# Retention and a low-rank mixer on one core: seven products for batch 1's second layer, fifteen sections instead of sixteen, another order in the front

## The chip, the cores and the metric

The kernel runs on one core of one Trainium2 chip. The metric is the device time of one execution, in microseconds. Before the change it is 306.77 us, the median of 3 runs (305.24 to 308.22). The names of the engines in the profile: PE is TensorE, PEld its weight load, DVE is VectorE, ACT is ScalarE, POOL is GpSimd, SP is SyncE, which here only starts DMAs.

## The reference

Eight batches, eight heads, 576 positions, head dimension 64, all float32. First a retention layer (attention without softmax, with a decay for each head), then a mixer over the sequence and a two-layer network over the channels:

```python
scores = scale * np.matmul(q, k.transpose(0, 1, 3, 2))
Dmat = np.where(rel >= 0, gamma[:, None, None] ** rel[None, :, :], 0.0)
x = np.matmul(scores * Dmat[None], v)            # then heads side by side: (8, 576, 512)
...
h = x.transpose(0, 2, 1) @ U @ V                 # rank 32, over the sequence
u = x + h.transpose(0, 2, 1)
out = u + np.maximum(u @ w_ch1, 0.0) @ w_ch2     # 512 -> 2048 -> 512
```

## The kernel before

**Chunks.** Two batches have 1152 rows, nine chunks of 128; the fifth chunk of such a pair (number J = 4) holds the last 64 rows of the even batch and the first 64 of the odd one. `order` numbers all 36 chunks of the four pairs, 0 to 35. The program calls a batch `b`, its pair `pr` and its place in the pair `par`.

**Retention.** The decay is folded into q and v by two scales, so a chunk needs its own masked scores and a running state. Chunks 0 to 8 (batches 0 and 1) are made by hand in `front`, in "units" of 256 rows with on-chip transposes: `cast_u` and `scale_u` bring q, k and v to bf16, `T_pe` transposes on TensorE, `T_cp` copies the result out of PSUM, `SC_u` makes scores, `mask_u` masks them, `RV_u` and `QS_u` make the output, `XS_u` scales it into the tile x. Chunks 9 to 35 go through a pipeline: `load` (SyncE queue, into the pool `stage` of 15 buffers; a chunk takes three), `prep` (cast of k, scale of q and v, and a transposing DMA on SyncE's queue), and then a **section**. `section(new, last)` makes the scores and the state increments of the chunks of group `new` and the outputs of the group before (`last`): four lists of 64x64 matmuls, lines 319, 336, 405 and 416. After it come `mask` (line 355: three operations on VectorE for a group of two chunks, four for one) and `cast_states` (line 384).

**Mixer.** `mixer_items` makes U and V products (`MA`, `MH`) and adds them to x as u; `MT` transposes u.

**Network.** Y1 (line 559) multiplies u by w1 in blocks of 128 columns with four matmuls of up to 512 columns each, and ScalarE takes the ReLU. Y2 (line 765) makes a chunk of 128 rows by 16 matmuls of 128x512, VectorE adds u (line 771) and GpSimd's queue stores it. Where `parted` is true (today pairs 1 to 3), four chunks are taken together and split in halves in every direction, and Y2's eight half-size products become seven (Strassen's scheme, in Winograd's form): `product` in `y2_items` (line 810), 16 matmuls of 128x256 for each. They need eight sums S of parts of y1 (`s_sum`, line 739) in every batch and eight sums T of parts of w2 (`t_sums`, line 599) once, all on VectorE, and corrections afterwards: `after` copies a bank on ScalarE (line 828), adds on VectorE (847, 854) and adds u on GpSimd (line 832). Banks A, B and C live in the three-buffer pool `ps_big`, which Y1, sections and the mixer use too. An odd batch keeps its chunk J as a whole chunk.

**Order.** Nothing is scheduled by a planner: the program runs under `manual_schedule`, each engine takes its instructions in the order in which the program issues them. `front` is written out. From then on a batch's main work is a list of items with costs (Y1 and Y2 items, in TensorE columns), and `merge` (line 16) issues steps between them: `plan[b]` gives a letter and a share of the batch's cost for each step. S is a section, M its mask, C its cast of states, L the loads of a chunk's k and q, K of its v, P (and Q, O) its preparation with k cast on GpSimd (VectorE, ScalarE), W and V a swap of v, G a mixer item, A an S sum, T a T sum, R and X sums for the last batch, F a pair of rows of w2 (`gated_w2`, which waits for a block of y1). Batch 1's list begins with what `front` leaves of Y1 (ten blocks) and then holds Y2 of batch 0 and of batch 1:

```python
main = y1_left + y2_items(0, 0) + y2_items(0, 1)
```

`groups` (line 1483) says how many chunks each section takes: (1, 2, 2, 1, 2, 1) and then twice (2, 2, 1, 2, 2), sixteen groups for 27 chunks.

Of the kernel before, what the change touches and what calls it, by code (L numbers as in the profile page):

```python
# [30 lines left out]
def kernel(  # L31
# [17 lines left out]
    P = 128  # L49
# [667 lines left out]

    P_ORDER = ((0, 0), (1, 0), (0, 1), (1, 1), (2, 0), (2, 1), (3, 0), (3, 1))
# [23 lines left out]
    def y2_items(pr, par):  # L742
# [47 lines left out]
        def product(n, e):  # L790
# [10 lines left out]
                4: ("A", False, y[:, hi, c + 2 * P:c + 4 * P],  # L801
# [15 lines left out]
        def after(n):  # L817
# [7 lines left out]
            copied = {1: ("A", lo[:, :, L]), 6: ("A", lo[:, :, H_]), 5: ("C", hi[:, :, H_])}  # L825
            if n in copied:
                bank, to = copied[n]
                nc.scalar.activation(out=to, in_=st[bank], func=AF.Copy)  # L828
# [24 lines left out]
            if n == 4:  # L853
                nc.vector.tensor_tensor(
                    out=hi[:, :, L], in0=st["A"], in1=u_hi[:, :, L], op=ALU.add)
            if last_b and n == 4:
                store(hi, L, nc.sync)
            elif not last_b and n in (3, 4):
                store(lo if n == 3 else hi, slice(0, dm), nc.gpsimd)

        parted = pr > 0
# [7 lines left out]
        if parted:  # L869
            for n in (1, 2, 6, 5, 7, 3, 4):  # L870
# [356 lines left out]
    def front():  # L1227
# [77 lines left out]
        cast_J(HI, POOL, (1,))  # L1305
        cast_J(HI, POOL, (0,))
        load_w1(2)
# [75 lines left out]
        T_cp(2, 1, DVE)  # L1383
        T_pe(2, 0)
        T_cp(2, 0, DVE)
        ys[7]()
# [7 lines left out]
        ys[9]()  # L1394
        cast_u(3, 1, 0, POOL)
        cast_u(3, 1, 1, POOL)
        load_w1(3)
        cast_u(3, 0, 0, POOL)
        cast_u(3, 0, 1, POOL)
        load(*order[NI], (1, 0, 2), gate=True)  # L1400
        load(*order[NI + 1], (1, 0, 2))
        scale_u(3, 0, POOL)
        scale_u(3, 1, POOL)
        T_pe(3, 1)
        T_cp(3, 1, DVE)
        ys[10]()
# [11 lines left out]
        load(*order[NI + 2], (1, 0, 2))  # L1418
        load_w2(0)
        load_w2(2)  # L1420
        load_w2(4)
# [7 lines left out]
        warm(3, ps_big, "big")  # L1429
        MA1(steps=(0, 3))  # L1430
# [7 lines left out]
        XS_u(3, 1, 2)  # L1438
        to_xT(1, (0, 1), (5, 6))
        ys[14]()  # L1440
        to_xT(1, (0, 1), (7,))
        MA1(steps=(3, J))
# [9 lines left out]
        prep(NI)  # L1452
# [24 lines left out]
    with tc.manual_schedule():  # L1477
# [5 lines left out]
        for size in (1, 2, 2, 1, 2, 1) + 2 * (2, 2, 1, 2, 2):  # L1483
# [120 lines left out]
```

## Time and profile before

| | |
|---|---|
| median of 3 runs | 306.77 us (305.24 to 308.22) |
| profiled execution | 306.29 us |
| its span, first to last instruction | 304.5 us |
| granted TensorE clock | 1.000 |
| DMA, mean over the span | 175 GB/s, 53.35 MB |
| queue of SyncE, share of 16 engines' time | 62.5% |
| queue of GpSimd, the same | 16.0% |
| chain that ended last | PE 88%, DMA 7%, SyncE's queue 3% |
| batch 2's first Y1 matmul starts | 105.57 us |

A row of a group reads: line, engine, operation, tiles (out<-in), shape, how many | busy time, mean ns of one | idle time of the engine just before them, and who ended it. A row of the timeline reads: start, duration of the run of equal instructions, engine, line, operation, tiles, shape, count, and in brackets the wait before it. The chain's rows are start, duration, what, count. Matmuls are pipelined, so a mean duration of one is longer than the spacing of two; the spacing is read from runs of equal matmuls.

### The profile page before, as it was taken

The numbers are of one execution on the slowest core, as the hardware profiler recorded it, in microseconds if no ns is written. First come the engines' busy times: TensorE is split into PE (matmuls) and PEld (weight loads), VectorE is DVE, ScalarE is ACT, GpSimd is POOL, SyncE is SP. The second block draws the span as 40 slices with busy tenths as digits, with TensorE's granted clock in tenths as the row PEclk, the third lists the DMA queues.
The fourth block names the chain that finished last, engine by engine and source line by source line (L and its number), as shares of the span: only waits on it lengthen the run. The fifth ranks groups of instructions, "written<-read, shape, count | busy, mean of one in ns | idle before, by whom it ended". The sixth has DMA issues, their size and how long they took to land.

```text
span 304.5 us, 9953 instructions
## 1 busy us (share of the span) xinstructions
PE 296.6 (97%) x4268; PEld 197.9 (65%) x4276; DVE 209.0 (69%) x373; ACT 156.4 (51%) x321; POOL 139.4 (46%) x173
## 2 busy tenths in 40 slices
PE   8799999999999999999999999999999999999996
PEld 3565564554554444887768845887758745887885
DVE  7863764633678986889269487787589528867763
ACT  3647456662424286447872376367842375226510
POOL 6672864463264475437620486259342400550130
PEclk9999999999999999999999999999999999999999
DMA  6999899999999999899978699959774033030013
GB/s 198 284 189 260 238 203 219 202 232 195 269 211 255 247 243 215 151 177 301 220 157 166 147 230 205 196 136 297 139 167 111 5 140 86 2 125 15 1 54 121
DMA packets 150268, 53.35 MB, mean 175 GB/s; under 512 B 128880, under 2 KB 148208, under 8 KB 150224
## 3 DMA queue, kind: packets, MB, share of 16 engines
q1 hardware_dynamic: 143616, 40.40, 62.5%
q0 software_dynamic: 6608, 12.32, 16.0%
q8 instruction: 33, 0.54, 0.7%
q14 instruction: 11, 0.09, 0.1%
HBM read 36.85 MB, written 9.44 MB: 152 GB/s over the span
## 4 chain that ended last, share of the span: by engine, by line
PE 88%; DMA 7%; SPq 3%; issue 1%; POOL 0%; DVE 0%; POOLq 0%
PE ps_y L559 34%; PE ps_A L810 14%; PE ps_y L765 12%; PE ps_C L810 7%; PE ps_B L810 3%; DMA stage_t<-in_q_dram 3%; PE ps_yA L680 3%; SPq L1220 2%; DMA stage_t<-in_v_dram 2%; DMA stage_t<-in_k_dram 2%; PE po L405 2%; PE psc L319 1%; PE po L416 1%; PE ph L497 1%; PE ps_y L780 1%; PE ps_yC L680 1%
## 5 line engine op out<-in xcount | busy, mean ns | idle before, releaser
L559 PE MATMUL ps_y<-uT,w 128*128 128x512 bf16 (+3 forms) x632 | 111.6, 331 | 0.0
L565 ACT ACTIVATE y<-ps_y 128x512 bf16<-128x512 f32 (+3 forms) x158 | 75.6, 500 | 40.3 <-PE ps_y L559 39.8
L559 PEld LDWEIGHTS <-w 128*128 128x128 bf16 x632 | 57.4, 98 | 42.6 <-issue 0.5
L832 POOL TENSOR_TENSOR o_lo<-o_lo,u 128x512 f32<-128x512 f32 x12 | 17.4, 1452 | 61.8 <-DVE o_lo L847 41.5
L810 PEld LDWEIGHTS <-S 128*128 128x128 bf16 x384 | 37.0, 98 | 4.7
L765 PE MATMUL ps_y<-w_sb,y 128*128 128x512 bf16 x168 | 38.4, 379 | 0.8 <-issue 0.6
L265 POOL TENSOR_TENSOR qk<-stage_t,qscale 128x512 bf16<-128x512 f32 x27 | 28.7, 1064 | 20.0 <-DMA stage_t<-in_q_dram 17.7
L275 POOL TENSOR_TENSOR vt<-stage_t,vscale 128x512 bf16<-128x512 f32 x27 | 29.7, 1098 | 15.6 <-DMA stage_t<-in_v_dram 14.5
L739 DVE TENSOR_TENSOR S<-y 128x1024 bf16<-128x1024 bf16 x24 | 20.6, 864 | 18.3 <-ACT y L565 18.3
L355 DVE TENSOR_TENSOR ret<-psc,triX 64x512 bf16<-64x512 f32 (+2 forms) x53 | 31.0, 585 | 1.0
L810 PEld LDWEIGHTS <-y 128*128 128x128 bf16 x288 | 27.8, 98 | 4.1
L765 PEld LDWEIGHTS <-y 128*128 128x128 bf16 x176 | 16.5, 98 | 19.2
L503 DVE TENSOR_TENSOR u<-ph,xt 128x512 bf16<-128x512 f32 (+4 forms) x33 | 22.4, 733 | 5.5 <-PE ph L497 5.2
L425 ACT ACTIVATE xt<-po 128x512 bf16<-128x512 f32 x27 | 14.9, 595 | 20.1 <-PE po L416 19.7
L377 DVE TENSOR_TENSOR s_f<-inc,s_f 128x256 f32<-128x256 f32 x38 | 16.1, 424 | 10.7 <-PE inc L336 9.0
L810 PE MATMUL ps_A<-T,S 128*128 128x256 bf16 x192 | 23.3, 273 | 0.0
L828 ACT ACTIVATE o_lo<-ps_A 128x512 f32<-128x512 f32 x12 | 7.2, 597 | 28.2 <-PE ps_A L810 23.6
L384 ACT ACTIVATE s_sb<-s_f 128x1024 bf16<-128x1024 f32 (+1 forms) x16 | 14.7, 921 | 8.9 <-DVE s_f L377 8.1
L1017 POOL CAST qk<-stage_t 128x512 bf16<-128x512 f32 (+1 forms) x21 | 13.4, 639 | 12.5 <-DMA stage_t<-in_k_dram 12.5
L1017 DVE COPY vs<-vt 64x256 bf16<-64x256 bf16 x32 | 15.5, 486 | 0.5
L832 POOL TENSOR_TENSOR o_hi<-o_hi,u 128x512 f32<-128x512 f32 x6 | 7.1, 1176 | 14.8 <-DVE o_hi L847 14.2
L905 POOL CAST qk<-stage_t 128x512 bf16<-128x512 f32 x16 | 9.7, 617 | 8.7 <-DMA stage_t<-in_k_dram 5.9
(173 smaller groups left out, 430.3 us busy)
## 6 DMA issues: line engine op xcount, KB each, us to landing
stage_t<-in_q_dram SPq DMA_DIRECT2D x32, 256.0 KB
stage_t<-in_k_dram SPq DMA_DIRECT2D x30, 256.0 KB
stage_t<-in_v_dram SPq DMA_DIRECT2D x30, 256.0 KB
out_dram<-o_lo POOLq DMA_DIRECT2D x5, 512.0 KB, 4.5
out_dram<-o_hi POOLq DMA_DIRECT2D x5, 512.0 KB, 5.5
w<-in_moe_w_ch_dram POOLq DMA_DIRECT2D x4, 512.0 KB, 7.6
w_sb<-in_moe_w_ch_dram POOLq DMA_DIRECT2D x8, 256.0 KB, 6.0
out_dram<-o POOLq DMA_DIRECT2D x8, 256.0 KB, 3.7
```

The lines of the kernel that those rows point to most:

```text
L265: nc.gpsimd.tensor_tensor(out=t[:, 0, :].rearrange("p (h d) -> p h d", d=D), in0=c["f", 0], in1=qscale[:, i, :, None].to_broadcast([P, H, ...
L275: (eng or nc.gpsimd).tensor_tensor(out=c["v"][rows], in0=c["f", 2][rows], in1=vscale[rows, i, :, None].to_broadcast([n, H, D]), op=ALU.mult,)
L355: nc.vector.tensor_tensor(out=ret[to, n, 0:m], in0=psc[rows, bank, 0:m * D].rearrange("p (b i) -> p b i", i=D), in1=tri_m[rows], op=ALU.mult,)
L377: nc.vector.tensor_tensor(out=s_f[:, s, :], in0=src, in1=s_f[:, st["f_end"], :], op=ALU.add)
L503: nc.vector.tensor_tensor(out=st["u", par][:, i0 - base:i0 - base + n, w].rearrange("p s (c d) -> p c s d", c=len(ccs)), in0=t[:, :, 0:n, ...
L559: nc.tensor.matmul(ps[:, 0:n, :], w1_t[f * P // W1B][:, cc, f * P % W1B:f * P % W1B + P], st["uT", par][:, c0:c0 + n, cc, :], start=(cc == ...
L565: nc.scalar.activation(out=st["y1", par][:, f, c0 * P:(c0 + n) * P], in_=ps[:, 0:n, :].rearrange("p s t -> p (s t)"), func=AF.Relu)
L739: nc.vector.tensor_tensor(out=t[:, k, js], in0=in0, in1=in1, op=op)
L765: nc.tensor.matmul(ps, st["y1", par][:, f, c * P:(c + 1) * P], w2_sb[:, f, :], start=(f == 0), stop=(f == NF - 1),)
L810: nc.tensor.matmul(st[bank][:, e, :], a[:, j, e * P:(e + 1) * P], w(j), start=(first and e == 0 and j == 0), stop=True, skip_group_check=True,
L832: nc.gpsimd.tensor_tensor(out=o[:, :, w], in0=o[:, :, w], in1=u[:, :, w], op=ALU.add)
L1017: eng.tensor_copy(out=out, in_=in_)
```

## The change

1. **Sections.** The group sizes become (1, 2, 2, 1), six times 2, and (2, 2, 1, 2, 2): fifteen groups. Chunks 17 and 18, which were in two groups, form one.
2. **Batch 1's Y2 in seven products.** `parted` becomes true for `par == 1` of pair 0. There the order of products is 1, 2, 4, 6, 5, 7, 3 instead of 1, 2, 6, 5, 7, 3, 4 (`early4`): product 4 goes to a bank D of its own, which ScalarE copies out, and is added after product 7. Batch 1 gets eight S sums (A steps, order `P1_ORDER`); the T sums start at the head of its plan and end before product 7, in another order.
3. **Front.** One load of w1 (`load_w1(2)`) is issued one cast earlier on GpSimd, `load_w1(3)` two casts earlier; `ys[7]` and `ys[10]`, blocks of four Y1 matmuls of batch 0, go ahead of transposes; unit 3's scales go ahead of the gated loads of chunk 9; `warm(3)` becomes `warm(2)`; the mixer's first three steps move behind unit 3's outputs; chunk 9's `prep` comes earlier, and the loads of w2 rows 2 to 5 and of chunk 11 come behind it.
4. **Steps at other places.** The plans of batches 1 to 7 are new.

```diff
+    P1_ORDER = ((0, 0), (1, 0), (0, 1), (1, 1), (2, 0), (2, 1), (3, 0), (3, 1))
...
-                4: ("A", False, y[:, hi, c + 2 * P:c + 4 * P],
+                4: ("D" if early4 else "A", early4, y[:, hi, c + 2 * P:c + 4 * P],
...
+            if early4:
+                copied[4] = ("D", hi[:, :, L])
...
-            if n == 4:
+            if early4 and n == 7:
+                nc.vector.tensor_tensor(
+                    out=hi[:, :, L], in0=st["A"], in1=hi[:, :, L], op=ALU.add)
+                add_u(hi, L, u_hi)
+            elif not early4 and n == 4:
...
-            elif not last_b and n in (3, 4):
+            elif not last_b and n in (3, 7 if early4 else 4):
...
-        parted = pr > 0
+        parted = pr > 0 or par == 1
+        early4 = pr == 0
...
-            for n in (1, 2, 6, 5, 7, 3, 4):
+            for n in (1, 2, 4, 6, 5, 7, 3) if early4 else (1, 2, 6, 5, 7, 3, 4):
...
+        load_w1(2)
         cast_J(HI, POOL, (0,))
-        load_w1(2)
...
+        ys[7]()
         T_pe(2, 0)
         T_cp(2, 0, DVE)
-        ys[7]()
         ys[8]()
...
+        load_w1(3)
         cast_u(3, 1, 0, POOL)
         cast_u(3, 1, 1, POOL)
-        load_w1(3)
         cast_u(3, 0, 0, POOL)
         cast_u(3, 0, 1, POOL)
+        scale_u(3, 0, POOL)
+        scale_u(3, 1, POOL)
         load(*order[NI], (1, 0, 2), gate=True)
         load(*order[NI + 1], (1, 0, 2))
-        scale_u(3, 0, POOL)
-        scale_u(3, 1, POOL)
+        ys[10]()
         T_pe(3, 1)
         T_cp(3, 1, DVE)
-        ys[10]()
...
-        load(*order[NI + 2], (1, 0, 2))
         load_w2(0)
-        load_w2(2)
-        load_w2(4)
...
-        warm(3, ps_big, "big")
-        MA1(steps=(0, 3))
+        warm(2, ps_big, "big")
         RV_u(3, 0)
...
         XS_u(3, 1, 2)
+        prep(NI)
+        load_w2(2)
+        load_w2(4)
+        load(*order[NI + 2], (1, 0, 2))
...
-        MA1(steps=(3, J))
+        MA1(steps=(0, J))
...
-        prep(NI)
         load_w2(6)
...
-        for size in (1, 2, 2, 1, 2, 1) + 2 * (2, 2, 1, 2, 2):
+        for size in (1, 2, 2, 1) + 6 * (2,) + (2, 2, 1, 2, 2):
...
-        t_order = [(k, half) for k in range(4) for half in range(2)]
+        t_order = [(k, half) for k in (0, 1, 3, 2) for half in range(2)]
...
-            sums = list(P_ORDER if b == B - 1 else S_ORDER) if pr else []
+            sums = list(P_ORDER if b == B - 1 else P1_ORDER if b == 1 else S_ORDER)
```

The plan of batch 1, where most of it happens, before and after:

```diff
-            1: ("F.039 Q.0726 S.118 L.1736 K.1753 W.1802 F.1823 W.1901 C.2583 P.2585 "
-                "Q.3063 L.3157 L.3468 M.3469 K.3698 V.4225 S.4276 K.434 O.4367 M.4856 "
-                "K.5071 P.5251 C.537 S.5581 M.5838 L.6099 W.6207 C.6783 T.6854 L.7 T.7065 "
-                "S.71 K.7122 P.7196 G.7368 M.745 T.7709 G.79 K.8049 T.8077 V.8107 T.8113 "
-                "T.8127 G.82 L.8681 C.886 S.8982 C.9003 M.9187 P.9275 T.9908 T.9999 L.9999"),
+            1: ("T.0 P.0589 F.0605 W.0983 S.0993 C.1498 T.1532 W.1651 L.1861 K.2046 F.235 "
+                "T.2987 Q.3063 L.3175 P.3195 K.32 K.3453 M.3662 T.3778 V.405 L.4124 T.4155 "
+                "S.4253 C.4565 L.4586 O.478 K.4803 M.4813 V.5075 T.5174 P.532 S.5364 L.5583 "
+                "M.5702 A.624 T.6291 K.6343 A.663 A.6639 C.6784 A.682 S.6961 M.7072 P.7167 "
+                "G.7711 K.7756 G.8009 C.8265 K.8283 A.8351 L.8393 A.8421 A.846 A.8584 "
+                "T.8796 S.8854 G.8872 L.8906 Q.9066 Q.9163 C.9228 V.9554"),
```

In batch 2's plan the first section stands at S.1186 (before: S.2131) and takes chunks 17 and 18.

39 rows, old and new, of the table plan are left out of this document.

## The prediction

> **What bounds the kernel now.** I read the page first, then who made TensorE wait, then the chain that ended last, and only then the other engines' rows at the places that the change touches.
>
> ```profile
> span 304.5 us, 9953 instructions
> ## 1 busy us (share of the span) xinstructions
> PE 296.6 (97%) x4268; PEld 197.9 (65%) x4276; DVE 209.0 (69%) x373; ACT 156.4 (51%) x321; POOL 139.4 (46%) x173
> ```
>
> ```profile
> PE pw L216 <- POOL ident masks.py:199: 1.4, 1, 1.4
> PE pst L920 <- POOL qk L905: 1.1, 3, 0.5
> PE ps_y L765 <- issue: 0.6, 4, 0.2
> ```
>
> The first fence says that TensorE is hardly ever free. The second is the list of its waits, longest first: one wait for the identity at the start, waits for casts in the front, and four gaps of about 0.16 us ahead of Y2's matmuls, which no other engine causes. So outside the front the order of TensorE's own instructions sets the end, and an edit is worth what it takes from, or adds to, that queue. What other engines do counts only once it is late.
>
> The chain (start, length, what, how many instructions) shows the two rates that matter, and what a section and the mixer's steps take:
>
> ```profile
> 33.10 1.73 PE ps_y L559 x8
> ...
> 90.57 0.30 PE po L405 x20
> 91.66 1.67 PE ps_y L765 x7
> 93.34 0.39 PE pa L461 x20
> 93.73 1.83 PE ps_y L765 x8
> 95.56 0.34 PE ph L497 x16
> ...
> 123.92 1.75 PE ps_B L810 x16
> ```
>
> Eight products of 128x512 take 1.73 us, 0.216 each (Y2's whole chunks have the same shape; some of their records are missing, so I take the rate from this row). Sixteen of 128x256 take 1.75 us, 0.109 each. A section with one new chunk lasts from 90.57 to 91.66, 1.1 us; the mixer's first product takes 0.39, its second 0.34.
>
> **Part 1: batch 1's Y2.** Today five chunks of 16 matmuls of 128x512. After: one such chunk, then seven products of 16 matmuls of 128x256. Removed: 64 x 0.216 = 13.8 us. Added: 112 x 0.109 = 12.2 us. TensorE saves 1.6 us. The four gaps before L765 stand after a section or a mixer step that interrupts a whole chunk; two of the four (the one ahead of 91.66, and the one behind the mixer's second product) lie in the part that becomes products, and L810's rows show no such gap, so I take off 2 x 0.16 = 0.3 more. Bounds: 1.6 to 2.0.
>
> The Trainium skill, TensorE: Matmul & The Clock Gate, section "Back-to-back issue gap", gives for a stream of weight loads and matmuls a sustained 131 ns at 512 columns and 81 ns at 128; worked out by it (an estimate, with some 98 ns at 256 between the two), 64 x 0.131 = 8.4 us would go and 112 x 0.098 = 11.0 us would come, and the change would cost 2.6 us. The rows above contradict it at both widths, and agree with the formula that the same section gives for a single gap; the rows decide.
>
> **What the seven products ask of VectorE.** They need eight sums S (line 739) in batch 1, and the eight sums T (line 599), which today end at 110 us, done before product 7.
>
> ```profile
> L739 DVE TENSOR_TENSOR S<-y 128x1024 bf16<-128x1024 bf16 x24 | 20.6, 864 | 18.3 <-ACT y L565 18.3
> ...
> L739 DVE TENSOR_TENSOR S<-y,S 128x1024 bf16<-128x1024 bf16 x12 | 8.0, 681 | 0.1
> ```
>
> ```profile
> 85.00:106.00 21.00, 20.63 (x302) 10.14 (x303) 18.29 (x34) 6.36 (x11) 10.60 (x15) 1.00 1.01 242
> ```
>
> In this stretch (columns: TensorE, weight loads, VectorE, ScalarE, GpSimd) VectorE is already busy for 18.3 of 21.0 us, six T sums among them. After the change six T sums leave it, two come back, eight S sums come: 18.3 - 4 x 0.68 (a T sum, next fence) + 8 x 0.8 (between the two forms' means) is about 22 us, for a stretch that TensorE wants to end 1.6 us sooner. So I walk VectorE's queue from batch 2's mixer step on:
>
> ```profile
> 96.50 2.42 DVE L503 TENSOR_TENSOR u<-ph,xt 128x1024 bf16<-128x1024 f32 x3
> 98.83 0.68 DVE L599 TENSOR_TENSOR T<-w_sb,T 128x1024 bf16<-128x1024 bf16 x1
> ...
> 102.32 1.87 DVE L377 TENSOR_TENSOR s_f<-inc,s_f 128x256 f32<-128x256 f32 x4 [0.40 <-PE inc L336]
> 104.11 2.09 DVE L355 TENSOR_TENSOR ret<-psc,triX 128x512 bf16<-128x512 f32 x3
> 106.22 0.69 DVE L771 TENSOR_TENSOR o<-ps_y,u 128x512 f32<-128x512 f32 x1
> 106.83 3.60 DVE L599 TENSOR_TENSOR T<-w_sb,T 128x1024 bf16<-128x1024 bf16 x2
> 110.35 0.74 DVE L1017 CAST qk<-stage_t 128x512 bf16<-128x512 f32 x2
> ```
>
> TensorE first. Section 3 ends at 91.66 today with 22 groups of Y2 done; in the new plan it stands after 20, two groups of 0.86 earlier, so product 1 starts near 89.9. Products 1, 2, 4, 6 and 5 (5 x 1.75), the mixer's 0.4 and 0.3 and a section of 1.1 among them: product 7 is reached near 100.5 and reads the last T sum in its fifth matmul, near 100.9. VectorE: the mixer's matmuls end near 95.0, its adds 2.4, four S sums 2.7, one T sum 0.7: 100.9, just in time. From there four states 1.9, two casts 0.7, three adds of 0.69, and the mask 2.1 end at 107.7; TensorE's next section starts near 107.4 (two products and four blocks of Y1 later) and needs the mask about 0.4 later. So nothing is lost while every sum takes 0.68, and nothing is spare.
>
> Sums don't always take 0.68. The two T sums at 106.83 took 3.60; GpSimd was then here:
>
> ```profile
> 107.82 1.06 POOL L265 TENSOR_TENSOR qk<-stage_t,qscale 128x512 bf16<-128x512 f32 x1
> 108.82 1.05 POOL L275 TENSOR_TENSOR vt<-stage_t,vscale 128x512 bf16<-128x512 f32 x1
> ```
>
> The second sum ended when both GpSimd operations had: 3.60 - 2 x 0.68 = 2.2 us of hold. The Trainium skill, SBUF — State Buffer, section "Who interferes with whom", says that a VectorE instruction with two SBUF inputs and a GpSimd instruction that reads SBUF exclude each other for a whole instruction; the trace agrees, and shows a price of two instructions in a row. GpSimd prepares chunks 17 and 18 exactly while those five sums are due. By form, the two sums S(2) carry 0.86 - 0.68 = 0.18 each over the plain duration, S(3) and T none: 0.4. With 0.1 because the two queues meet with nothing to spare I put **0.5 us** of TensorE waiting here; ends 0 (no meeting) and 4.5 (two holds).
>
> **Part 2: sections.** Sixteen groups become fifteen, but every chunk keeps its matmuls; what goes is a mask in four pieces and a cast off the path. TensorE: 0, ends -0.3 and +0.3 (two such gaps).
>
> **Part 3: the front.** Four Y1 matmuls move ahead of the transposes that wait for unit 2's queries, and four ahead of unit 3's.
>
> ```profile
> 31.86 0.28 PE L920 MATMUL pst<-ident,qk 128*128 128x128 bf16 x2 [0.15 <-POOL qk L905]
> 32.59 0.51 PE L920 MATMUL pst<-ident,qk 128*128 128x128 bf16 x6 [0.45 <-POOL qk L905]
> ```
>
> ```profile
> 33.13 1.31 DVE L1017 COPY qkT<-pst 128x1024 bf16<-128x1024 bf16 x1 [0.70 <-PE pst L920]
> ...
> 41.21 2.36 DVE L957 TENSOR_TENSOR ret<-psc,triU 128x1024 bf16<-128x1024 f32 x2
> ```
>
> ```profile
> 34.80 1.17 POOL L905 CAST qk<-stage_t 128x512 bf16<-128x512 f32 x2
> 35.91 0.80 POOL L220 DMA_DIRECT2D w<-in_moe_w_ch_dram  x1
> 36.71 1.18 POOL L905 CAST qk<-stage_t 128x512 bf16<-128x512 f32 x2
> ```
>
> The 0.6 us of waiting is filled, but the cast's end doesn't move, and the filler is then missing later: the scores need VectorE's copy (ends 34.44), and TensorE, with one block of four (0.86) instead of two behind the transposes' end at 33.1, is there at about 33.95, so 0.5 comes back. The next bound is GpSimd: the issue of w1's last quarter goes ahead of both pairs of casts, whose sum stays 1.17 + 0.80 + 1.18, so unit 3's queries are ready near 38.0 as today. What is behind that is the same in both orders. The warm-up matmul that goes (0.2) uncovers the first mask, which ends at 41.21 + 1.18 = 42.4, and three steps of the first mixer product move behind it. I put the front at **0**; ends -0.6 (the wait is really gone) and +0.6.
>
> **Part 4: what moved on the queues.** Chunk 9 (the first that a step of the plan uses) is prepared earlier, so two loads of w2 queue behind its values' landing on GpSimd, where they stood ahead of it:
>
> ```profile
> 50.01 1.04 POOL L275 TENSOR_TENSOR vt<-stage_t,vscale 128x512 bf16<-128x512 f32 x1 [3.83 <-DMA stage_t<-in_v_dram]
> ```
>
> They go out near 51. Y2 reads them only ten blocks of Y1 into batch 1; the first T sum, now at the head of that batch's plan, meets them first, and if it is late, VectorE's next work is the first section's states, four blocks further on, and nothing waits. On SyncE the transpose of chunk 9 now goes ahead of chunk 11's loads. The T tiles take slots of the 15 staging buffers from the head of that batch on, so loads may wait longer for one. In batches 2 to 7 no instruction is added; TensorE shows no wait there now. All this: 0, ends 0 and +1 without that cover.
>
> **Sum** against the profiled execution's own 306.29 us (span 304.5 and 1.8 around it; 0.5 below the median of 306.77): 306.3 - 1.6 - 0.3 + 0.5 = **304.9 us**.
>
> **The rivals.**
>
> *TensorE alone.* No sum meets GpSimd, and a part of the front's wait goes: 306.3 - 1.9 = 304.4, and with 0.6 of the front and 0.3 of the sections 303.5. For it: no wait of TensorE outside the front. Against: VectorE has no spare time from 95 to 108. Chance 0.22.
>
> *VectorE and GpSimd collide* in batch 1's products. One hold in place of the mean's 0.4: 304.9 - 0.4 + 2.2 = 306.7; a second, at chunk 18: 308.9; a third ahead of the mask: 311. From 1.8 us of holding on the gain is gone. For it: the 3.60 row, and two preparations at that place. Against: S(3)'s twelve sums show no hold. Chance 0.16.
>
> *A late chunk.* Chunk 18's scores, now in batch 2's first section, are due at 108 instead of in the middle of batch 2. Its keys are cast behind those sums, near 103.9, and two transposes follow on one queue:
>
> ```profile
> 104.40 1.70 SPq L283 DMA_TRANSPOSE qkT<-qk  x1
> ```
>
> 103.9 + 2 x 1.7 = 107.3, then the landing: under 1 us to spare. Another transpose's time late gives 306.6. Chance 0.12.
>
> *The change doesn't do what it says:* the products would run at the whole chunk's rate per column with no work saved. The rates above exclude it; 0.01.
>
> **How the numbers follow.** My forecast, 303.9 to 306.0, has 0.49. 1% is 3.1 us, about what a measurement of this kernel can tell from no change: below 303.2 is faster, above 309.4 slower. Faster takes a third of "TensorE alone" and some for a front that gains more than I see: 0.15. Slower takes two holds or a late chunk with a hold: 0.11. The range, 302.8 to 308.4, leaves out the best front and the third hold.
>
> **What would show it.** Right: 112 matmuls at L810 in batch 1 at 1.75 us for 16; the gaps before L765 down from four to two; S sums near 87 to 101 us; batch 2's Y1 starting near 104.4 instead of 105.7; TensorE's new waits for VectorE small and in products 7 or the section after. Wrong: TensorE waiting over 1.5 us for S, T or a mask in that stretch; sums of over 1 us there; a wait at L319 for a transpose; or unit 2's and 3's transposes in the front ending over 0.6 us away from 33.1 and 38.

## The result, and the profile after

| | before | after |
|---|---|---|
| median of 17 runs each | 306.04 us (305.08 to 312.72) | 311.29 us (308.17 to 313.84) |
| ratio after/before | | 1.0153, 95% interval 1.0131 to 1.0175 |
| profiled execution, span | 306.29 us, 304.5 | 310.09 us, 308.2 |
| batch 1's Y1 tail starts (first matmul, line 559) | 55.97 | 59.15 |
| batch 2's Y1 | 105.57 | 107.99 |
| batch 3's Y1 | 136.66 | 140.04 |
| batch 4's, 5's, 6's Y1 | 174.14, 204.23, 241.57 | 177.33, 207.71, 245.19 |

The change makes the kernel slower; the forecast of 304.9 us, and its range up to 308.4, were wrong. The stages of the two profiled executions differ by +3.2 us in the front, -0.8 in batch 1, +1.0 in batch 2 and +0.3 in the rest. Here and below, medians are of all executions, while ratios and their intervals leave out those more than 1.5% above the fastest of the same kernel.

The page of the profile after, then who made TensorE wait from 30 us on (total, times, longest):

```profile
span 308.2 us, 10058 instructions
## 1 busy us (share of the span) xinstructions
PE 297.8 (97%) x4318; PEld 203.7 (66%) x4323; DVE 208.9 (68%) x372; ACT 159.0 (52%) x327; POOL 146.0 (47%) x176
```

```profile
PE pss L1015 <- POOL stage_t L249: 1.8, 1, 1.8
PE psc L319 <- DMA qkT<-qk: 0.7, 1, 0.7
PE psc L958 <- DVE qkT L1026: 0.5, 1, 0.5
PE ps_y L766 <- issue: 0.3, 2, 0.2
```

(Lines after: Y2 is 766, the products 811, S sums 740; the rest shifts likewise.) TensorE is busy for 1.2 us more, although the change was to take work out, so what was lost is partly slow work. The gaps ahead of Y2 went from four to two, as forecast. Two waits are new: one in the front, and one at line 319, where a section waits for a chunk's transposing DMA.

**The front's wait.** GpSimd's timeline (start, duration, what; in brackets the wait before it):

```profile
34.53 0.80 POOL L220 DMA_DIRECT2D w<-in_moe_w_ch_dram  x1
35.33 2.27 POOL L914 CAST qk<-stage_t 128x512 bf16<-128x512 f32 x4
37.61 1.05 POOL L918 TENSOR_TENSOR qk<-stage_t,vscaleU 128x512 bf16<-128x512 f32 x1
41.98 1.06 POOL L918 TENSOR_TENSOR qk<-stage_t,vscaleU 128x512 bf16<-128x512 f32 x1 [3.31 <-DMA stage_t<-in_v_dram]
```

The casts of unit 3 end in time, as forecast, but the second half of its values lands only at 41.9, 3.3 us after GpSimd was ready for it. TensorE stands still from 41.26 to 43.08, and then its clock is halved (the column ahead of the last two is the granted clock):

```profile
42.00:44.00 2.00, 0.92 (x26) 0.49 (x25) 0.75 (x2) 0.48 (x2) 1.84 (x5) 1.00 0.00 0
44.00:46.00 2.00, 2.00 (x28) 1.29 (x28) 0.89 (x1) 0.27 (x1) 0.00 (x0) 0.70 0.83 175
46.00:48.00 2.00, 2.00 (x21) 0.73 (x19) 0.53 (x1) 0.60 (x1) 0.00 (x0) 0.50 1.24 245
```

From 42 to 44 no DMA moves anything (share 0.00): the next loads on SyncE wait for the memset at line 249, which stands behind the late scale on GpSimd. (SyncE waits 7.9 us for it, and chunk 9's loads go out at 43.09 instead of 37.94 before.) So the late values cost 1.8 us of standing, and more at half speed.

**Chunk 14's transposing DMA.** SyncE's queue, before and then after:

```profile
75.34 0.58 SPq L255 DMA_DIRECT2D stage_t<-in_k_dram  x1
...
78.86 2.36 SPq L255 DMA_DIRECT2D stage_t<-in_v_dram  x2
81.34 1.98 SPq L283 DMA_TRANSPOSE qkT<-qk  x1
```

```profile
80.48 2.61 SPq L255 DMA_DIRECT2D stage_t<-in_k_dram  x1
83.14 0.79 SPq L255 DMA_DIRECT2D stage_t<-in_q_dram  x1
83.97 1.48 SPq L255 DMA_DIRECT2D stage_t<-in_k_dram  x1
85.50 0.85 SPq L255 DMA_DIRECT2D stage_t<-in_q_dram  x1
86.46 3.15 SPq L283 DMA_TRANSPOSE qkT<-qk  x1
```

The DMA at 81.34 before and at 86.46 after is chunk 14's. After, k and q of chunks 15 and 16 (1 MB) are issued between 80.48 and 86.35, and the transpose stands behind them. The chain of after shows the price (start, length, what):

```profile
80.48 5.95 DMA stage_t<-in_k_dram
86.46 6.72 DMA qkT<-qk
93.22 0.32 PE psc L319 x16
...
93.67 1.85 PE ps_A L811 x16
...
106.29 1.75 PE ps_C L811 x16
108.03 2.06 PE ps_y L559 x9
```

Load and transpose need 5.95 and 6.72 us here from issue to landing. That they need about the same agrees with the Trainium skill, Advanced Engine Details and Errata, section "DMA Advanced Topics", which has transposing DMAs on this chip as fast as plain ones; what costs is the queue. The product stretch itself, 93.67 to 108.03, is 14.4 us, and VectorE goes through it in the order of my walk:

```profile
99.01 2.42 DVE L503 TENSOR_TENSOR u<-ph,xt 128x1024 bf16<-128x1024 f32 x3 [0.96 <-PE ph L497]
101.35 1.28 DVE L740 TENSOR_TENSOR S<-y 128x1024 bf16<-128x1024 bf16 x2
102.55 1.29 DVE L740 TENSOR_TENSOR S<-y,S 128x1024 bf16<-128x1024 bf16 x2
103.75 0.69 DVE L599 TENSOR_TENSOR T<-w_sb 128x1024 bf16<-128x1024 bf16 x1
```

No sum is held up in this execution: each takes 0.6 to 0.7. In most of the later kernels a pair of them is, as is shown below.

### The profile page after: what moved, and what is told of

It is laid out like the page before. It is cut to its first block, busy times and chain, and to the rows that moved or that the text cites. A ratio compares the mean times of both kernels' runs of the same rounds, so it can differ in the third digit from the quotient of the medians.

```text
span 308.2 us, 10058 instructions
## 1 busy us (share of the span) xinstructions
PE 297.8 (97%) x4318; PEld 203.7 (66%) x4323; DVE 208.9 (68%) x372; ACT 159.0 (52%) x327; POOL 146.0 (47%) x176
## 4 chain that ended last, share of the span: by engine, by line
PE 68%; DMA 18%; SPq 9%; POOL 2%; issue 1%; DVE 1%; ACT 0%; POOLq 0%
PE ps_y L559 25%; PE ps_A L811 15%; PE ps_C L811 8%; DMA stage_t<-in_q_dram 8%; DMA stage_t<-in_v_dram 4%; SPq L255 4%; PE ps_B L811 4%; DMA stage_t<-in_k_dram 4%; SPq L1229 3%; PE ps_yA L680 3%; PE ps_y L766 2%; DMA qkT<-qk 2%; PE po L405 1%; PE psc L319 1%; PE ps_y L781 1%
## 5 line engine op out<-in xcount | busy, mean ns | idle before, releaser
L836 POOL TENSOR_TENSOR o_lo<-o_lo,u 128x512 f32<-128x512 f32 x14 | 20.8, 1488 | 64.2 <-DVE o_lo L851 44.0
L811 PEld LDWEIGHTS <-S 128*128 128x128 bf16 x448 | 43.1, 98 | 5.9 <-issue 0.3
L265 POOL TENSOR_TENSOR qk<-stage_t,qscale 128x512 bf16<-128x512 f32 x27 | 30.5, 1130 | 12.6 <-DMA stage_t<-in_q_dram 9.1
L740 DVE TENSOR_TENSOR S<-y 128x1024 bf16<-128x1024 bf16 x28 | 24.0, 867 | 17.3 <-ACT y L565 17.1
L811 PEld LDWEIGHTS <-y 128*128 128x128 bf16 x336 | 32.0, 98 | 5.0 <-issue 0.4
L811 PE MATMUL ps_A<-T,S 128*128 128x256 bf16 x224 | 26.9, 273 | 0.0
L766 PE MATMUL ps_y<-w_sb,y 128*128 128x512 bf16 x107 | 24.4, 380 | 0.5 <-issue 0.3
L766 PEld LDWEIGHTS <-y 128*128 128x128 bf16 x112 | 10.6, 98 | 12.3
L836 POOL TENSOR_TENSOR o_hi<-o_hi,u 128x512 f32<-128x512 f32 x8 | 9.2, 1156 | 14.8 <-DVE o_hi L851 14.4
L1024 ACT ACTIVATE vs<-vt 64x256 bf16<-64x256 bf16 x26 | 10.8, 414 | 7.7 <-PE po L416 6.0
L811 PE MATMUL ps_C<-w_sb,S 128*128 128x256 bf16 x112 | 14.0, 273 | 0.0
```

The costliest lines, as they stand in the source:

```text
L265: nc.gpsimd.tensor_tensor(out=t[:, 0, :].rearrange("p (h d) -> p h d", d=D), in0=c["f", 0], in1=qscale[:, i, :, None].to_broadcast([P, H, ...
L740: nc.vector.tensor_tensor(out=t[:, k, js], in0=in0, in1=in1, op=op)
L766: nc.tensor.matmul(ps, st["y1", par][:, f, c * P:(c + 1) * P], w2_sb[:, f, :], start=(f == 0), stop=(f == NF - 1),)
L811: nc.tensor.matmul(st[bank][:, e, :], a[:, j, e * P:(e + 1) * P], w(j), start=(first and e == 0 and j == 0), stop=True, skip_group_check=True,
L836: nc.gpsimd.tensor_tensor(out=o[:, :, w], in0=o[:, :, w], in1=u[:, :, w], op=ALU.add)
```

## The experiments

Two theories stood at the start. The front's (A, where the texts use letters): unit 3's values are late because w1's last quarter is issued ahead of the casts, and that is the loss. The plan's (C): the loads and transposing DMAs of batches 1 and 2 run late in their new order. None of the kernels leaves work out. They ran on four chips, each beside before on its own chip; after was not run again beside them, so they are compared with it by their ratios. All results:

| kernel | median us (lowest to highest, runs) | ratio to before, 95% interval |
|---|---|---|
| e1_w1_back | 311.3 (306.28 to 311.65, 4) | none given |
| e3_front_of_before | 309.79 (307.15 to 311.31, 4) | 1.0114, 1.0057 to 1.0171 |
| e4_front_alone | 306.19 (305.41 to 312.88, 10) | 1.0021, 0.9991 to 1.0051 |
| e5_warm | 309.48 (306.9 to 312.84, 4) | 1.0104, 1.0050 to 1.0159 |
| f1_prep14_first | 309.26 (306.14 to 314.25, 10) | 1.0046, 0.9998 to 1.0094 |
| f2_old_load_order | 312.27 (308.53 to 314.5, 4) | 1.0178, 1.0084 to 1.0273 |
| f3_no_products | 310.98 (310.77 to 315.72, 4) | 1.0174, 1.0145 to 1.0204 |
| f5_prep14_old_front | 307.88 (306.55 to 310.76, 6) | 1.0093, 1.0038 to 1.0149 |
| g1_products_alone | 313.15 (311.47 to 315.32, 6) | 1.0228, 1.0172 to 1.0284 |
| g4_prep18_earlier | 314.63 (313.64 to 316.75, 6) | 1.0290, 1.0241 to 1.0339 |
| h1_before_load16_early | 307.13 (304.77 to 312.2, 12) | 1.0022, 0.9986 to 1.0057 |
| h2_load16_behind | 309.6 (306.14 to 312.25, 12) | 1.0082, 1.0043 to 1.0122 |
| i1_uT_first | 310.17 (306.44 to 313.38, 12) | 1.0103, 1.0065 to 1.0141 |
| i2_T_first | 309.01 (307.3 to 311.75, 6) | 1.0106, 1.0050 to 1.0162 |
| i3_both_first | 309.05 (306.47 to 311.84, 11) | 1.0091, 1.0055 to 1.0126 |
| i4_both_old_front | 306.91 (305.94 to 310.88, 12) | 1.0034, 1.0001 to 1.0068 |

### The front: w1's quarter back, before's front in after, after's front in before, warm-up matmuls

```diff
-        load_w1(3)
         cast_u(3, 1, 0, POOL)
         cast_u(3, 1, 1, POOL)
+        load_w1(3)
```

> The changed kernel with one line moved: the load of w1's last quarter goes back behind unit 3's first two casts on GpSimd's queue. Theory A (that load, issued 1.4 us earlier and now together with unit 3's last value load, delays those values by some 4 us, so that TensorE waits 1.8 us at L1015 and then runs at half the clock): unit 3's last scale starts near 39 instead of 41.98, the wait and the half-clock stretch are gone, and the time falls by 3 to 4 us from 311.3, to a ratio of 1.000 to 1.006 against the kernel before. Theory B (it is the gated loads behind the scales, or another move in the front): the scale stays near 42, ratio 1.012 to 1.018. Theory C (new plans and products cost the time, not the front): ratio within 0.003 of 1.015.

Next, the function `front` of before in place of the changed one, and the reverse, the changed `front` in before:

> The changed kernel with the whole front of the kernel before; sections, products and plans are the new ones. Theory A or B (the front holds the whole loss and more): batch 1's Y1 tail starts near 56.0 instead of 59.15, the ratio is 0.994 to 1.002, and the late chunk 14 (0.7 us at L319) goes or stays without mattering much. Theory C (plans and products cost the time): 1.008 or more.

> The kernel before with the new front alone; sections, products and plans are the old ones. Theory A or B: the wait at the states of unit 3 and the half-clock stretch are there as in the changed kernel, +3.2 us at batch 1's Y1 tail, ratio 1.010 to 1.016. Theory C: 1.000 to 1.004.

The fourth adds matmuls ahead of the step that had waited:

```diff
         mask_u(3, 0)
+        warm(9, ps_big, "big")
         ST_u(3, LO, acc[2], False)
```

> The changed kernel with nine more warm-up matmuls (1.94 us at full rate) ahead of the states of unit 3, where TensorE would wait; the computation is the same. If the idle stretch is what lowers the granted clock, the wait is filled, the clock in the front stays at 1.00, matmuls at 44 to 48 us are spaced 0.216 instead of 0.43, and the time falls by about 1.6 us from 311.3, ratio about 1.010. If the lower clock has another cause (a limit that comes by itself), the clock falls all the same and the ratio stays at 1.015 or rises to 1.016.

The front's theory falls as the whole cause: with before's front the changed kernel stays 1.1% slower, and the changed front alone in before costs 0.2%, with no change inside the interval. With w1's quarter back the late values are gone from the profile (unit 3's last scale ends at 39.4), but section 3 then waits 1.9 us at line 319, and the median is that of after (one execution of four took 306.28). Theory A's mechanism holds as far as the profiles go: where w1's last quarter goes first (eleven kernels), GpSimd waits 1.0 to 3.3 us for those values in five and 0.7 at most in six; where it goes behind the casts (seven), 0.5 at most. In the profile with before's front the waits sit in the plan; TensorE's longest (the three at line 319 are in different sections):

```profile
PE psc L319 <- DMA qkT<-qk: 3.0, 3, 1.5
PE ps_y L559 <- DMA uT<-u: 1.1, 1, 1.1
```

With warm-up matmuls the ratio is the expected 1.010, though its interval reaches into that of after. The clock in the front stays at 1.00 in the profile, and the mean clock of all four executions is 0.999 or more. The profiled one (306.9 us, span 305.1; the other three took 308.6 to 312.8) happened to have nothing in the plan late: from 57 us on TensorE's longest wait is 0.2. Its front still ends 1.5 us later than before's, and unit 3's values were 1.8 us late. It shows what the changed plan takes when nothing in it is late; its chain:

```profile
91.14 1.85 PE ps_A L811 x16
...
103.77 1.75 PE ps_C L811 x16
105.51 3.45 PE ps_y L559 x16
```

Batch 1 takes 47.90 us in it (57.45 to 105.35, first Y1 matmul to first Y1 matmul), against 49.60 before: the products are worth 1.7 us. Batches 2 to 5 take 136.85 against 136.00, so 0.85 of that is given back later. (This difference is steady: with before's plan two other profiles take 135.95 and 136.02, with the changed sections none takes less than 136.8.)

### Chunk 14's preparation ahead of the loads

```diff
-"T.2987 Q.3063 L.3175 P.3195 K.32 K.3453 M.3662 T.3778 V.405 L.4124 T.4155 "
-"S.4253 C.4565 L.4586 O.478 K.4803 M.4813 V.5075 T.5174 P.532 S.5364 L.5583 "
+"T.2987 Q.3063 L.3175 P.3195 K.32 K.3453 M.3662 T.3778 V.405 O.4123 L.4124 T.4155 "
+"S.4253 C.4565 L.4586 K.4803 M.4813 V.5075 T.5174 P.532 S.5364 L.5583 "
```

> After with one step of batch 1's plan moved: chunk 14's preparation (cast, scales, transposing DMA) stands ahead of the loads of k and q of chunks 15 and 16 on SyncE's queue instead of behind them. Queue theory (the late section is made by the order on that queue): the transposing DMA is issued near 82 instead of 86.5, section 3 no longer waits at L319 and batch 1 is 1 to 2 us shorter, so 1.000 to 1.008 of before's time. Rival (the queue and the DMA engines are simply full, and the front hands over 1 to 3 us late): the wait moves to the section of chunks 15 and 16, the sum stays, 1.012 to 1.018.

And the loads of chunks 15, 16 and 17 where before had them (15 at .3607, chunk 14's O at .4542, 16 at .6342, 17 at .716):

> After with the loads of k and q of chunks 15, 16 and 17 and the preparation of chunk 14 at the fractions of batch 1 where before had them (15 earlier, 16 and 17 later), everything else as after. Queue theory: as in the other kernel with the preparation moved, no wait at L319 for chunk 14, 1.000 to 1.008, and a later chunk may wait instead since its load is later (at most 1 us). Rival (staging buffers are short because the T tiles take them from the start of batch 1): chunk 15's load now stands in the queue for a buffer, and the stretch from 75 to 95 us stays as late as in after.

Both take the wait at line 319 away. In the first the queue reads:

```profile
76.69 1.45 SPq L255 DMA_DIRECT2D stage_t<-in_v_dram  x2
78.79 1.31 SPq L283 DMA_TRANSPOSE qkT<-qk  x1
80.15 0.59 SPq L255 DMA_DIRECT2D stage_t<-in_k_dram  x1
```

The ratio falls from 1.0153 to 1.0046, but five of ten runs are still above 309, and the median of all ten, 309.26, is 1.1% above before's 305.96 on that chip. Behind the mended wait the next ones stand. In its chain batch 2's u, and its transposing DMA, now set the end of batch 1:

```profile
97.13 1.74 DVE S L740 x2
98.86 5.98 DMA uT<-u
104.84 0.14 issue
104.98 1.24 PE ps_y L559 x5
```

In the old order of loads, product 7 waits 1.2 us for T and batch 2's Y1 1.0 for VectorE's last addition; with four runs it can't be told from after. So to take the wait at line 319 away was not enough there. VectorE has little room left: from 75 to 95 us (the third engine of the row, after TensorE and its weight loads) it is busy for 13.51 us before and 18.04 after.

```profile
75.00:95.00 20.00, 19.52 (x389) 10.31 (x390) 13.51 (x27) 7.45 (x13) 8.73 (x13) 1.00 1.01 242
```

```profile
75.00:95.00 20.00, 18.99 (x374) 10.54 (x375) 18.04 (x33) 7.06 (x12) 10.62 (x14) 1.00 1.15 227
```

And here VectorE's sums do meet GpSimd. With chunk 14 first, a pair of S sums takes 2.13 us instead of 1.28 while GpSimd scales a chunk's values:

```profile
97.04 2.13 DVE L740 TENSOR_TENSOR S<-y 128x1024 bf16<-128x1024 bf16 x2
```

```profile
97.40 1.22 POOL L275 TENSOR_TENSOR vt<-stage_t,vscale 128x512 bf16<-128x512 f32 x1 [0.90 <-DMA stage_t<-in_v_dram]
```

In the old order of loads a pair takes 2.98 us, and GpSimd's two scales of a chunk stand inside it. In eleven of the fourteen profiles with products in batch 1 a pair takes 1.6 to 3.0 us, each time with a GpSimd scale beside it; TensorE then waits 0.3 to 1.2 us for T in six of the eleven.

### No products, and before's front with chunk 14 mended

```diff
-        parted = pr > 0 or par == 1
+        parted = pr > 0
```

(with batch 1's eight A steps gone and its fractions scaled to the longer list)

> After with batch 1's Y2 as whole chunks again (no products, no S sums and no additions in batch 1; the T tiles still early; the plan's fractions scaled so that its steps stay at the same work). If the seven products save what the sum said (1.6 of TensorE time and 0.3 of gaps), this is 1.5 to 2.2 us slower than after: 1.020 to 1.023 of before. If they bring nothing because the VectorE work behind them costs as much, it equals after, 1.013 to 1.017; if that VectorE work is what makes after slow, it is faster than after, 1.005 or less.

And the function `front` of before in the kernel with chunk 14's preparation first:

> Both the front of before and chunk 14's preparation ahead of the loads of chunks 15 and 16, the rest as after. Queue theory: front as in before, section 3 on time, the 1.9 us of the products come out: 0.994 to 1.002 of before. Rival (full queue): 1.008 to 1.012 as with the front of before alone, with waits at L319 at other chunks.

Without products the kernel is as slow as with them, though batch 1 itself takes 49.6 us, 1.7 more than the 47.9: the wait has moved to batch 2's first section, the place that my rival of a late chunk had named. Its longest wait:

```profile
PE psc L319 <- DMA qkT<-qk: 2.2, 1, 2.2
```

So my three outcomes for this kernel were too simple: how long the products take doesn't set the time while a chunk is late anyway. Before's front with chunk 14 mended, at 1.0093, lies in the rival's range, but without the rival's waits: line 319 has none in its profile, and the longest is 0.6 us for VectorE's last addition.

### Products alone in before, and chunk 18 earlier in after

The first keeps before's front, sections and loads and adds only the products with their sums, at after's fractions (batch 1's plan is before's, scaled to the shorter list, with after's T and A steps). Two of its edits:

```diff
-        parted = pr > 0
+        parted = pr > 0 or par == 1
+        early4 = pr == 0
```

The second moves chunk 18's load and the preparations of chunks 17 and 18, on top of chunk 14's:

```diff
-"G.7711 K.7756 G.8009 C.8265 K.8283 A.8351 L.8393 A.8421 A.846 A.8584 "
-"T.8796 S.8854 G.8872 L.8906 Q.9066 Q.9163 C.9228 V.9554"),
+"G.7711 L.7755 K.7756 G.8009 C.8265 K.8283 A.8351 A.8421 A.846 A.8584 "
+"T.8796 S.8854 Q.8855 G.8872 Q.8902 L.8906 C.9228 V.9554"),
```

> Before's front, sections, loads and preparations, and of the change only batch 1's seven products with what they need: the T tiles from the head of batch 1, the eight S sums, the P1 order and the additions at after's fractions. Theory that chunks are late (two-chunk sections in a row and the new queue order): no section waits for a transposing DMA, batch 1 is 1.5 to 1.9 us shorter, 0.993 to 0.996 of before. Rival (the T tiles take staging buffers and so make the loads late, or VectorE lags behind products 3 and 7): waits at L319 or at the first L559 of batch 2, 1.000 to 1.012.

> After with chunk 14's preparation ahead of the loads of chunks 15 and 16, and also the load of chunk 18 and the preparations of chunks 17 and 18 moved earlier in batch 1. If the second late place is chunk 18 in batch 2's first section, the runs near 310 that the kernel with chunk 14 alone still had become rare: 0.998 to 1.004 in the median. Rival (the lateness sits at many places, since every section of two chunks needs its second chunk a section sooner): the runs still scatter from 306 to 312, 1.004 to 1.012.

Both missed, on the slow side. In the first, GpSimd's timeline shows why; ScalarE's row follows:

```profile
95.40 1.16 POOL L836 TENSOR_TENSOR o_lo<-o_lo,u 128x512 f32<-128x512 f32 x1
105.29 2.27 POOL L836 TENSOR_TENSOR o_hi<-o_hi,u 128x512 f32<-128x512 f32 x2 [8.73 <-DVE o_hi L851]
...
108.61 0.71 POOL L1026 CAST qk<-stage_t 128x512 bf16<-128x512 f32 x1
```

```profile
111.36 0.84 ACT L1024 ACTIVATE vs<-vt 64x256 bf16<-64x256 bf16 x2 [4.55 <-POOL vt L275]
```

GpSimd stands 8.7 us at the products' addition of u, chunk 17's preparation is queued behind it, ScalarE waits for that chunk's values with Y1's ReLU queued behind, and TensorE waits 3.3 us for a PSUM bank, besides 1.6 for T. So in before's order of preparations the products lose more than they save. In the second, SyncE waits for the cast that was moved ahead, and batch 2's u stands behind it:

```profile
98.19 1.86 SPq L255 DMA_DIRECT2D stage_t<-in_v_dram  x2
105.17 1.23 SPq L283 DMA_TRANSPOSE qkT<-qk  x1
106.50 1.63 SPq L515 DMA_TRANSPOSE uT<-u  x1
```

Batch 2's Y1 waits 4.1 us. A transpose moved ahead of its data held back what stands behind it in the queue, here for 5.1 us (100.05 to 105.17).

### The queue's order from both sides

```diff
-"Q.3063 L.3157 L.3468 M.3469 K.3698 V.4225 S.4276 K.434 O.4367 M.4856 "
-"K.5071 P.5251 C.537 S.5581 M.5838 L.6099 W.6207 C.6783 T.6854 L.7 T.7065 "
+"Q.3063 L.3157 L.3468 M.3469 K.3698 V.4225 S.4276 K.434 L.4366 O.4367 M.4856 "
+"K.5071 P.5251 C.537 S.5581 M.5838 W.6207 C.6783 T.6854 L.7 T.7065 "
```

> Before, with one step moved: the load of k and q of chunk 16 stands ahead of chunk 14's preparation in batch 1, as in the changed plan, instead of behind chunk 15's. Nothing else changes. Queue theory: the transposing DMA of chunk 14 is issued 2 to 4 us later than before's 81.3, some 84 to 86, and lands at the start of section 3 (91.0): a wait of 0 to 2 us there, 1.002 to 1.012 of before. Rival (the lateness comes from the two-chunk sections or the products, before has room): no wait at L319, 0.998 to 1.002.

```diff
-"S.4253 C.4565 L.4586 O.478 K.4803 M.4813 V.5075 T.5174 P.532 S.5364 L.5583 "
+"S.4253 C.4565 O.478 L.4781 K.4803 M.4813 V.5075 T.5174 P.532 S.5364 L.5583 "
```

> After, with the load of k and q of chunk 16 moved behind chunk 14's preparation and everything else where it is, the preparation too. Queue theory: two transfers of 256 KB leave the front of the transposing DMA, which is issued near 83.5 (the cast that feeds it ends at 83.8 in after's trace) instead of 86.5; section 3 does not wait; 1.003 to 1.009 of before, as with the preparation moved itself. Rival (only an earlier cast helps, or the lateness is spread over many places): 1.011 to 1.018, as after.

Two transfers in front of the transpose don't hurt before (the rival's outcome: chunk 14's goes out at 81.9, which is 7.6 us ahead of its section at 89.5). In after the same two transfers do matter: behind the transpose they leave 1.0082, with the transpose at 83.41 and no wait at line 319. With all four in front the transpose went out at 86.46, 86.83 and 86.74 in the three profiles where section 3 waits (after, w1's quarter back, before's front); with the same order it went out at 84.06 with warm-up matmuls, and nothing waited. So this order leaves too little room, and whether it costs depends on how late the queue already is.

### What is late next

On top of chunk 14's preparation first: batch 2's transposed u ahead of chunk 18's loads, the last T sum ahead of the last two S sums, both together (this diff), and both with before's front.

```diff
-"G.7711 K.7756 G.8009 C.8265 K.8283 A.8351 L.8393 A.8421 A.846 A.8584 "
-"T.8796 S.8854 G.8872 L.8906 Q.9066 Q.9163 C.9228 V.9554"),
+"G.7711 K.7756 G.8009 C.8265 K.8283 A.8351 G.8392 L.8393 A.8421 T.8459 A.846 A.8584 "
+"S.8854 L.8906 Q.9066 Q.9163 C.9228 V.9554"),
```

> After with chunk 14's preparation ahead of the loads of chunks 15 and 16, and with the transposing DMA of batch 2's u (line 515) ahead of the loads of chunk 18 on SyncE's queue instead of behind them. If that transfer is what takes back the rest (it is issued at 98.9, lands at 105.0 and batch 2's first Y1 waits 0.73 for it), it is issued 1 to 2 us earlier, the wait is gone and the time falls by 0.5 to 1 us against the kernel with chunk 14 alone: 1.000 to 1.003. Rival (VectorE's T tile ahead of product 7, or lateness that moves on to chunk 18): 1.004 to 1.010.

> After with chunk 14's preparation moved as before, and with the last T difference ahead of the last two S sums on VectorE. If VectorE's order is what takes back the rest (product 7 waits 0.33 for T in the profile with chunk 14 alone, 1.2 in the one with the old order of loads), that wait is gone and batch 1 is 0.3 to 1 us shorter: 1.001 to 1.004. Rival (the transposing DMA of batch 2's u sets the end of batch 1 anyway): no change, 1.004 to 1.010, the wait at batch 2's first Y1 grows by what the other loses.

> Both of these together. If the two are the whole rest: batch 1 takes 47.9 us as in the one execution in which nothing was late, the span is 303 to 304, 0.995 to 0.999 of before. Rival (the rest is spread over batches 2 to 6 and the front): 1.002 to 1.010.

> The same with the front of before. If the front's late values (1.5 to 1.8 us in some executions) are part of the scatter: 0.4 to 0.8 us below the kernel with the front of the change and fewer runs above 309. Rival (the front costs nothing on the median, as it did by itself): the same time within 0.3%.

The first takes its wait away in the profile (u's transpose goes out at 97.32 instead of 98.86), the second the one for T, but the times don't move: 1.0103, 1.0106 and 1.0091 cannot be told apart, nor from the 1.0082 above, and their intervals reach into that of chunk 14 alone (0.9998 to 1.0094). With before's front on the same chip the ratio falls from 1.0091 to 1.0034, more than expected, but the intervals overlap. The other such pair, chunk 14 alone, goes the other way by its ratios (1.0046 to 1.0093) and the same way by its medians (309.26 to 307.88). So a cost of the front of about 0.6% together with the new plan is likely, and not shown. In the profile with the change's front and both moves, TensorE waits for w2. The chain names the load: the last one, a step F of the plan, which stands at .235 (before: .1823).

```profile
PE ps_y L766 <- DMA w_sb<-in_moe_w_ch_dram: 1.1, 1, 1.1
```

```profile
64.81 7.23 DMA w_sb<-in_moe_w_ch_dram
```

No version with the products beats before; the best of them, before's front with all three orders mended, is 0.3% slower (0.0 to 0.7).

## Why the prediction was wrong

**Part 1 was right.** Its 1.9 us of saved matmuls and gaps are 1.7 in the execution with nothing late in the plan, and batch 1 takes 1.7 longer again without products. The product stretch takes 14.4 us there as in after, and the gaps are two.

**VectorE's walk was right, and so was its mechanism.** In after's own profile the sums ran at 0.6 to 0.7 and GpSimd met none of them. In eleven of fourteen profiles one or two scales met a pair, for 0.3 to 1.7 us of VectorE, and TensorE waited 0.3 to 1.2 us for T in six of them (1.6 with the products alone, where no sum was held). That is about the 0.5 us of the forecast, and "nothing is spare" held.

**Part 2 was mis-sized.** I put the sections at 0, with ends of 0.3. Batches 2 to 5, where TensorE's other work is the same, take 0.85 us more in the execution with nothing late (in 0.3 of it TensorE is idle). Their steps also stand at other places; neither that nor a section's size was tried by itself, so the cause of the 0.85 stays open.

**Part 3 looked at casts, not at what lands.** Unit 3's casts end when I said, and alone the front costs nothing, as forecast. But "what is behind that is the same in both orders" left out the values that follow: in after's profile they came 3.3 us after GpSimd was ready for them, and the front took 3.2 us more where I had put 0 (ends -0.6 and +0.6). That is one execution: in the other profiles with the changed front batch 1's Y1 tail starts at 55.0 to 58.2, not 59.15, and with before's front the changed kernel still loses 1.1%.

**Part 4 is the step that failed.** "All this: 0, ends 0 and +1". I saw that loads might wait longer and then took TensorE's lack of waits today as cover, without asking how near each transposing DMA was to its section. I priced a transposing DMA by its issue, 1.7 us; to its landing those in the chains of that stretch take 5.7 to 6.7 us. Chunk 14's, behind four transfers, made section 3 wait 0.7 us in after and 1.9 and 1.5 with w1's quarter back and with before's front. It is the largest single piece found: moving it, or two of the loads, takes the ratio from 1.015 to between 1.005 and 1.011 (by medians of all runs, from 1.017 to between 1.010 and 1.014). With before's front and the two other orders besides, it is 1.0034. So what Parts 3 and 4 put at 0 holds about 1.2% of the time, some 3.6 us of the loss; how that divides among the moves is not settled.

**The rivals.** *A late chunk* had the right mechanism, a wait at line 319, at the wrong place: it named chunk 18, which was late only in the profile without products, and 1.7 us. *Doesn't do what it says* is excluded by the rows above. *Collide* happened in eleven profiles, at less than its price of 2.2 us a hold, but not in after's own, which was slow without it. Had nothing been late, my 304.9 us and the 304.4 of *TensorE alone* would both have been near: the stages of the profile with warm-up matmuls, set behind before's front, end at 55.97 + 247.68 = 303.65, so about 305.4 us with the 1.8 around the span.

**What stays open.** Behind chunk 14's wait and the front, waits of 0.3 to 1.5 us come up at varying places (T, batch 2's u, w2), from one execution of a kernel to the next. The times without a profile can't be attributed to them, and the last 0.3% has no cause shown. One thing is on record for every execution, its mean granted clock. It is 0.995 or less in 16 of the 17 executions of after, in about a quarter of some 90 of before, in 14 of the 51 of f1, h2, i1, i2 and i3 (chunk 14 mended, the change's front), and in none of 4 with warm-up matmuls. At 0.994 a span of 308 us loses about 1.8 us. So a part of after's loss is slow clock in nearly every execution; which stop brings it there, the front's or section 3's, is not shown.

## What to carry to other kernels

Where an in-order DMA queue is full, price each moved load by everything that then stands behind it, and a transfer by its landing, not by its issue. For each transfer that TensorE will need, write down how long before its use it lands; an engine that shows no wait may have half a microsecond of room or five. A saving of 1.7 us in the bound engine brought all these dates forward by as much, and here not every one of them had that room.

## What the hardware showed

TensorE's clock falls to 0.50 in pieces of about 3.4 us, after short stops, but not after each. (Below, 4.00 us at a mean of 0.57 lack 1.7 us, which is 3.4 us at 0.50.) The stop of 1.82 us in after (from 41.26) was followed by 3.4 us at half clock (0.89, 0.50, 0.50, 0.50, 0.90 in the five microseconds from 44 on), the 2.19 us in the kernel without products by 3.4, the 3.27 us in the kernel with products alone by 6.8. The 1.94 us at section 3 with w1's quarter back, and the 1.49 us with before's front, were followed by none. One stretch each of the two kernels without products and with products alone:

```profile
113.00:117.00 4.00, 4.00 (x20) 1.53 (x12) 3.60 (x7) 0.98 (x2) 2.74 (x3) 0.57 1.09 247
```

```profile
112.00:118.00 6.00, 5.12 (x12) 1.61 (x11) 1.52 (x2) 2.97 (x6) 4.64 (x5) 0.50 1.03 260
```

The Trainium skill, TensorE: Matmul & The Clock Gate, section "🎯 Why this matters for your kernels", asks for no gaps over some 3 us. The traces show that a shorter one can do it, and that 3.4 us at half clock add 1.7 us to the stop.
